# Two grouped-query attention blocks on one core: six K and three V buffers, a wq load moved behind x, 105 remainder tiles transposed by DMA

## The chip, the cores and the metric

The kernel runs on one core of a Trainium2 chip. The metric is the device time of one execution in microseconds (us), as the median of several runs; lower is better.

## The reference

Two independent problems, A and B, have the same shapes: x is (16, 80, 576), wq (576, 4096), wo (4096, 576), and the K and V caches are (16, 16, 512, 128), all bf16. There are 32 query heads on 16 key and value heads, so two query heads share each K and V.

```python
q = (x @ wq).reshape(B, Sq, Hq, Dh).transpose(0, 2, 1, 3)
k = jnp.repeat(k_cache, 2, axis=1); v = jnp.repeat(v_cache, 2, axis=1)
scores = jnp.einsum("bhqd,bhkd->bhqk", q, k) * (Dh ** -0.5)
p = softmax(scores)
o = jnp.einsum("bhqk,bhkd->bhqd", p, v)
y = o.transpose(0, 2, 1, 3).reshape(B, Sq, Hq * Dh) @ wo
# output: concatenate([y_A, y_B], axis=-1)
```

## The kernel before, in words

**Units.** The attention is cut into 128 units U, 64 for each problem. A unit is one batch element and four key heads, and needs one K load and one V load of 512 KB each. Each key head has 2 x 80 = 160 query rows: 128 of them make a main score tile of 128x512, and the 32 left over of all four heads together make a fifth one, the remainder tile. So a unit has five tiles, k = 0 (remainder) to 4.

**The way of a tile.** On TensorE (PE): scores (L713, or L699 for the remainder, which is made for two units at once: 0, 1, then 2 and 3, 4 and 5, and so on); on DVE the negated row maximum (L722); on ACT the exponential with its row sum (L726); on DVE the reciprocal (L732); on POOL the scaling of the probabilities (L735). Then the tile is transposed, on PE by four 128x128 transposes (L741) with a copy out of PSUM (L748 and L750), or, for the remainder tile of the units in the table RSEL, by one DMA transpose from SBUF to SBUF (L754), with no work on PE or DVE. PV (L788, 16 matmuls a unit) multiplies with V, and ACT copies the result into oT (L804).

**Around it.** The query projection (L589) works in octets of eight units; wq comes in slices of 1024 columns, in two buffers. x of problem A is loaded as it stands (L492, four loads: x00 and x01 for the first half of the batch, x10 and x11 for the second) and transposed on PE (L507); x of problem B comes transposed by DMA (L527). The first two wq slices are loaded in two halves each (w00, w01, w10, w11; each half is a 64 KB and a 512 KB load, L560 and L563). The output projection (L841) gathers over pairs of slices, in acc and then into the output (L853, L869, L875).

**What sets the order.** A planner in the kernel (`_Sched`) runs when the kernel is built. Each operation has a stream, a key that is its due time, a duration and, for loads, a cost; `arrange` walks through planned time and gives each engine a fixed list. The chip then follows these lists, with semaphores for what is needed. For the first loads the planner uses landing times from the table LAND; later it models two queues. An operation with `after` does not start, in the plan, before the PV of a given mark (mark 4U + j is the j-th PV group of unit U) has, plus `lag`.

**Queues.** SP issues all loads of K (L663, DMA transposes), x, wq and wo, the remainder transposes (L754) and the stores (L875). ACT issues the V loads from V 4 on (L667). The order of the first loads on SP is the tuple FIRST, then x10, x11, v2 and v3 in LATER.

**Buffers.** K U sits in buffer U modulo NK, V U in U modulo NV, the transposed probabilities in one of NPT = 3. A load waits until PE has read the buffer's last content.

The lines that matter to the loads:

```python
S.add("sp", ... else 5.0 * gfirst[U] + 0.5 * (U - gfirst[U]) - LA - KK, em_ldk, writes=[R(("kT", ks), U)],
      ... after=4 * U - KPH if U >= KU0 else None, ...)
S.add(VENG if U >= NVS else "sp", ... else 5.0 * U - VK, em_ldv, ...
      lag=VLAG if U >= NVS else 0.0, after=... 4 * U - VPH if U >= VU0 else None, ...)
```

Of the kernel before, what the change touches and what calls it, by code (L numbers as in the profile page):

```python
# [11 lines left out]
GRP = (1, 1, 2)  # L12
GR = 2
LA = 13
NK = 5
NV = 4
NPA = 10
NPR = 5
NPT = 3
# [2 lines left out]
QL1 = 11.0  # L22
KC = 2.1
VK = 8.0
KK = 8.0
DLAT = 0.6
XC = 0.4
QL2 = 10.3
VC = 1.75
# [7 lines left out]
NWARM = 8  # L37
NWARM2 = 2
QP1 = (0.4, 1.1)
FIRST = ("x00", "w00", "x01", "w01", "k0", "w10", "k1", "v0", "k2", "k3", "v1", "w11", "k4")  # L40
LATER = dict(x10=-0.40, x11=-0.39, v2=-0.38, v3=-0.37)
LAND = dict(x00=4.1, w00=6.4, x01=8.0, w01=9.6, k0=11.5, w10=14.6, k1=18.1, v0=19.4, k2=21.8, k3=23.7, v1=26.4, w11=28.1,
            k4=30.3, k5=33.0, x10=35.7, x11=36.9, v2=38.0, v3=39.5, k6=43.2, k7=46.8)
NFK = 5
PTX = (0,)
NPX = 128
QEV = {160: dict(act=0.21, dve=0.24), 320: dict(act=0.32, dve=0.40), 480: dict(act=0.43, dve=0.57)}
NWC = 4
BANKS = dict(S=(0, 1, 2, 6), T=(3, 4), O=(5, 7), M=(7, 5), M0=(7, 5, 6, 3, 4), M1=(7, 6), ML=(7, 5, 6, 0, 1))
# [1 line left out]
VENG = "act"  # L51
VDUR = 0.42
VN = 1
VLAG = 2.0
VPH = 11
VU0 = 14
KPH = 27
KU0 = 10
KLAG = 0.0
XM = dict(wo=6.0, wq=6.0, wqb=6.0, RT=4.0, V=2.0, K=2.0, x=3.0)  # L60
# [2 lines left out]
WENG = "sp"  # L63
WOENG = "sp"
WLAG = 2.0
NVS = 4
QLAT = 1.25
QRING = 1.45
WOC = 1.05
XDMA = True  # L70
RG = (((0, 1, 2, 3, 4),), ((0,), (1, 2, 3, 4)))
RSEL = ((14, 15, (0, 1, 2, 3)), (17, 45, (0, 1, 2, 3)), (47, 48, (0, 1, 2, 3)), (49, 50, (0, 1, 2, 3)), (51, 52, (0, 1, 2, 3)), (53, 54, (0, 1, 2, 3)), (55, 56, (0, 1, 2, 3)), (57, 58, (0, 1, 2, 3)), (59, 76, (0, 1, 2, 3)), (77, 78, (0, 1, 2, 3)), (79, 80, (0, 1, 2, 3)), (83, 84, (0, 1, 2, 3)), (85, 88, (0, 1, 2, 3)), (89, 119, (0, 1, 2, 3)), (120, 121, (0, 1, 2, 3)), (122, 123, (0, 1, 2, 3)), (124, 128, (0, 1, 2, 3)))
RDC = 0.72
RDK = 2.0
RDO = 10.0
# [13 lines left out]
LPC = 29.0  # L89
WOR = (((4.0, 1.5), (12.0, 1.5)), ((7.0, 1.6), (15.6, 1.6)), ((8.0, 1.7), (16.0, 1.7)), ((9.0, 1.7), (16.0, 1.4)))  # L90
WQR = (2.0,3.5,9.5)
WQX = {9: (5.0, 2.0), 13: (4.0, 2.0)}
XR = ((-12.0, 1.9), (-9.5, 1.6))

MM0 = 0.0025
MM1 = 1.0 / 2400.0
# [274 lines left out]
def bass_concat_heads__gqa_block_cached__gqa_block_cached__near_ridge_kernel(  # L371
# [27 lines left out]
    with ExitStack() as es:  # L399
# [6 lines left out]
        kT = sb("kT", [128, NK, 4, 512], BF16)  # L406
# [24 lines left out]
        S = _Sched()  # L431

        def R(res, ver):
            return (res, ver)
# [33 lines left out]
        def em_warmend(e):  # L468
# [5 lines left out]
              stream="warmset")  # L474
# [12 lines left out]
        for half in range(NPP):  # L487
            x_ap = probs[0][0]
            for part, (k0, k1) in enumerate(XP):
                def em_ldx(e, x_ap=x_ap, half=half, k0=k0, k1=k1):  # L490
                    src = x_ap.rearrange("b s d -> (b s) d")[half * NROW + k0 * 128:half * NROW + k1 * 128, :]
                    return e.dma_start(xs[:, half * NRT + k0:half * NRT + k1, 0:D],  # L492
                                       src.rearrange("(k p) d -> p k d", p=128))

                S.add("sp", FIRST.index("x%d%d" % (half, part)) - 100.0 if half == 0 else LATER["x%d%d" % (half, part)], em_ldx,
                      writes=[R(("xs", half * NRT + k_), 0) for k_ in range(k0, k1)], dsem="d_x%d%d" % (half, part), land=LAND["x%d%d" % (half, part)],
                      name="ldx%d.%d" % (half, part), stream="later" if half else "first", dur=0.5, cost=XC * (k1 - k0))
            for blk in range(NRT):
                rb = half * NRT + blk
                vb = S.bank("M0" if half == 0 else "M1")  # L500
                x = (XA + 0.5 * blk if blk < 2 else XA + XB + 0.1 * blk) if half == 0 else XH + 0.8 * blk

                def em_xtr(e, rb=rb, vb=vb):
                    last = None
                    for ck in range(5):
                        c0 = ck * 128 if ck < 4 else D - 128
                        last = e.transpose(psb[:, vb.phys, ck * 128:(ck + 1) * 128], xs[:, rb, c0:c0 + 128], ident[:])  # L507
                    return last

                def em_xev(e, en=None, half=half, blk=blk, vb=vb):  # L510
                    return (e.copy if en == "act" or half == 0 and blk in (1, 3) else e.tensor_copy)(xT[:, half, :, blk * 128:(blk + 1) * 128],  # L511
                                         psb[:, vb.phys, 0:640].rearrange("p (c n) -> p c n", c=5))

                S.add("pe", x, em_xtr, reads=[R(("xs", rb), 0), IDENT], writes=[R(vb, 0)], name="xtr%d" % rb,
                      stream="X", dur=_mm(5, 128), lat=0.2, alloc=[vb])
                S.add(("act", "dve") if half else "act" if blk in (1, 3) else "dve", x + 0.3, em_xev, reads=[R(vb, 0)], writes=[R(("xT", half, blk), 0)],
                      name="xev%d" % rb, stream="xed" if half else "xea" if rb in (1, 3) else "xev",
                      dur=dict(act=0.52, dve=0.40), lat=0.13)

        for half in range(NPP):  # L520
            x_ap = probs[1][0]
            st0 = UPR + 16 * half - lead[NG // 2 + 2 * half]
# [16 lines left out]
        for goct in range(NG):  # L539
            prob, q, half = unit(goct)  # L540
# [4 lines left out]
            pieces = () if half else ((0, 512), (512, 1024)) if goct < 2 else ((0, 1024),)  # L545
            for pi, (c0, c1) in enumerate(pieces):
                st0 = u0 - lead[goct]
                t_ld = 5.0 * st0 - 20.0 if goct > 1 else FIRST.index("w%d%d" % (goct, pi)) - 100.0
                dsem = "d_wq%d" % wsl
                eng = "sp" if goct < 2 else WENG  # L550
                strm = "first" if goct < 2 else "wq"
                sp_ = st0 if goct < 2 else u0 - 16 - lead[goct - 2] + max(QSH, lead[goct - 2] - QS0)
                if goct < 2:
                    parts = ((4, 5, c0, c1), (0, 4, c0, c1))
                else:
                    parts = tuple((0, 4, 256 * j, 256 * j + 256) for j in range(4)) + ((4, 5, 0, 1024),)
                for j, (k0, k1, n0, n1) in enumerate(parts):
                    def em_ldw(e, wq_ap=wq_ap, q=q, wsl=wsl, n0=n0, n1=n1, k0=k0, k1=k1):
                        if k0 == 4:
                            return e.dma_start(wq_sb[64:128, wsl, 4, n0:n1],  # L560
                                               wq_ap[512:576, q * 1024 + n0:q * 1024 + n1])
# [12 lines left out]

# [79 lines left out]
        for U in range(NSU):  # L654
# [10 lines left out]
            def em_ldv(e, vc_ap=vc_ap, b=b, q=q, vs=vs):  # L665
                src = vc_ap[b:b + VN, 4 * q:4 * q + 4, :, :].rearrange("b g (p j) d -> p b g (j d)", j=4)
                return e.dma_start(v_sb[:, vs:vs + VN, :, :], src)  # L667

            S.add("sp", FIRST.index("k%d" % U) - 100.0 if U < NFK else 5.0 * gfirst[U] + 0.5 * (U - gfirst[U]) - LA - KK, em_ldk, writes=[R(("kT", ks), U)],
                  dsem="d_k%d" % ks, name="ldk%d" % U, stream="K" if U >= NFK else "first", dur=1.8, cost=KC, xp=True,  # L670
                  after=4 * U - KPH if U >= KU0 else None, lag=KLAG if U >= KU0 else 0.0, land=LAND.get("k%d" % U, 0.0))
            if U % VN == 0:
                S.add(VENG if U >= NVS else "sp", FIRST.index("v%d" % U) - 100.0 if U < 2 else LATER["v%d" % U] if U < NVS else 5.0 * U - VK, em_ldv, writes=[R(("V", vs + i_), U + i_) for i_ in range(VN)],
                      dsem="d_v%d" % vs, name="ldv%d" % U, stream="V" if U >= NVS else "later" if U > 1 else "first", dur=VDUR, cost=VN * VC,
                      lag=VLAG if U >= NVS else 0.0, after=VAF[U] if U < 4 else 4 * U - VPH if U >= VU0 else None,
                      land=LAND.get("v%d" % U, 0.0))

            vo = None
            rdma = any(a_ <= U < b_ and U % 4 in m_ for a_, b_, m_ in RSEL)
            for k in range(5):  # L680
# [91 lines left out]
                else:  # L772
                    S.add("pe", t0, em_tr, reads=[R(("P", psl), ("n", T)), IDENT], writes=[R(vt, 0)],
                          name="tr%d" % T, stream="T", dur=_mm(4, 128), lat=0.2, alloc=[vt])
                    free_ = k in PTX and U < NPX
                    S.add(("act", "dve") if free_ else "dve", t0 + 0.44, em_ptev, reads=[R(vt, 0)], writes=pt_writes,
                          name="ptev%d" % T, stream="ptex" if free_ else "ptev", dur=dict(act=0.50, dve=0.33), lat=0.13, ahead=PTO)

# [176 lines left out]
```

## Time and profile before

| | |
|---|---|
| runs | 764.65, 765.46 and 767.38 us; median 765.46 us |
| the profiled execution | 765.12 us; its span, first to last instruction, 763.4 us |
| TensorE clock granted | 1.000 |
| moved by DMA | 172.86 MB, mean 226 GB/s |
| K loads (L663) | 128; issue 3.58 us (A) and 3.19 us (B) median, landing 4.3 / 6.9 / 10.6 us |
| V loads (L667) | 128; landing 3.8 / 5.1 / 7.8 us |
| remainder transposes (L754) | 94; issue 1.21 us median, landing 2.4 / 4.9 / 8.4 us |

Landing is the time from the start of the issue to the end of the transfer, as minimum / median / maximum.

How to read it: the page's first part is the busy time of each engine with its share of the span and its count of instructions. A matmul's duration contains the drain of the array, which overlaps with the next one, so the pace is read from start to start in the order of time. A number in square brackets is the idle time of the engine before an instruction, followed by what ended it; where the engine named there had long been done, it was another, often a DMA. PEld is the weight load of TensorE, which overlaps with matmuls. SP's issue instructions are not counted as busy.

### The profile page before, as it was taken

To read this page: it belongs to the slowest core of one execution; us is meant where nothing else is said; L and a number is where in the kernel's file an instruction comes from. 1 tells how busy PE (TensorE), PEld (TensorE's weight loads), DVE (VectorE), ACT (ScalarE), POOL (GpSimd) and SP (SyncE) were. 2 spreads that over 40 slices of the span, in tenths; PEclk is the share of its full clock that TensorE was granted. 3 is DMA by queue.
4 is the path that set the end of the run, shared out by engine and by line. 5 is a ranking of instruction groups with operands and counts; after the bars stand their busy time and mean duration, and the time that the engine had idled before them with its cause. 6 is when DMAs were issued, how large, how long until landed. Compare 5 with 4: busy or idle time off the path is not lost.

```text
span 763.4 us, 21017 instructions
## 1 busy us (share of the span) xinstructions
PE 756.6 (99%) x7876; PEld 572.3 (75%) x7876; DVE 676.7 (89%) x1602; ACT 603.7 (79%) x1691; POOL 432.3 (57%) x647
## 2 busy tenths in 40 slices
PE   8999999999999999999999999999999999999998
PEld 4677777777777777777777777777777777777786
DVE  5999999998888898999989999889889989999982
ACT  3878988888888887787887878887888888877860
POOL 1646755656565565565656555655656565564660
PEclk9999999999999999999999999999999999999999
DMA  9999999999998999999999999999999999999751
GB/s 223 261 244 240 244 248 262 233 222 234 196 240 198 255 258 251 261 218 210 241 228 214 226 248 247 240 251 251 234 219 214 199 227 237 226 264 258 182 121 32
DMA packets 431364, 172.86 MB, mean 226 GB/s; under 512 B 327968, under 2 KB 430880, under 8 KB 431264
## 3 DMA queue, kind: packets, MB, share of 16 engines
q1 hardware_dynamic: 365712, 106.43, 78.4%
q10 hardware_dynamic: 65552, 65.09, 28.4%
q8 instruction: 64, 1.05, 0.6%
q14 instruction: 36, 0.29, 0.1%
HBM read 87.46 MB, written 2.95 MB: 118 GB/s over the span
## 4 chain that ended last, share of the span: by engine, by line
PE 97%; DVE 1%; ACT 1%; issue 0%
PE ps L589 23%; PE ps L841 21%; PE ps L788 18%; PE ps L741 16%; PE ps L713 14%; PE ps L699 5%; DVE negmax L722 1%; PE ps L461 0%; ACT p_sb L726 0%; PE ps L507 0%; DVE qT L601 0%; DVE xT L511 0%; ACT qT L600 0%; ACT xT L511 0%; DVE pT L750 0%
## 5 line engine op out<-in xcount | busy, mean ns | idle before, releaser
L735 POOL TENSOR_SCALAR p_sb<-p_sb,rinv 128x512 bf16<-128x512 bf16 x640 | 429.9, 692 | 308.9 <-DVE rinv L732 308.8
L726 ACT ACTIVATE p_sb<-ps,negmax 128x512 bf16<-128x512 f32 x640 | 440.9, 695 | 90.8 <-DVE negmax L722 81.4
L722 DVE TENSOR_REDUCE negmax<-ps 128x1 f32<-128x512 f32 x640 | 425.1, 680 | 17.0 <-PE ps L713 12.2
L788 PE MATMUL ps<-pT,v_sb 128*128 128x160 bf16 x2048 | 221.9, 233 | 0.0
L750 DVE COPY pT<-ps 128x512 bf16<-128x512 bf16 x512 | 206.1, 414 | 11.9 <-PE ps L741 11.2
L589 PE MATMUL ps<-xT,wq_sb 128*128 128x320 bf16 (+2 forms) x1280 | 213.5, 299 | 1.6 <-ACT xT L511 0.7
L741 PE MATMUL ps<-ident,p_sb 128*128 128x128 bf16 x2184 | 209.8, 219 | 0.0
L788 PEld LDWEIGHTS ps<-pT,v_sb 128*128 128x128 bf16 x2048 | 164.6, 98 | 47.7 <-issue 2.1
L713 PE MATMUL ps<-kT,qT 128*128 128x512 bf16 x512 | 193.4, 379 | 0.0
L741 PEld LDWEIGHTS ps<-ident,p_sb 128*128 128x128 bf16 x2184 | 155.1, 98 | 34.4 <-issue 5.1
L841 PE MATMUL ps<-wo_sb,oT 128*128 128x288 bf16 x1280 | 170.0, 286 | 0.0
L589 PEld LDWEIGHTS ps<-xT,wq_sb 128*128 128x128 bf16 x1280 | 116.0, 98 | 52.7 <-DVE qT L601 2.5
L841 PEld LDWEIGHTS ps<-wo_sb,oT 128*128 128x128 bf16 x1280 | 122.4, 98 | 34.6 <-issue 1.7
L804 ACT CAST oT<-ps 128x320 bf16<-128x320 f32 x256 | 109.0, 426 | 29.5 <-PE ps L788 27.9
L726 ACT ACTIVATION_READ_ACCUMULATOR p_sb<-ps,negmax 128x1 f32 x640 | 132.1, 206 | 0.0
L601 DVE TENSOR_SCALAR qT<-ps 128x320 bf16<-128x320 f32 (+2 forms) x158 | 76.5, 485 | 13.8 <-PE ps L589 11.1
L600 ACT ACTIVATE qT<-ps 128x320 bf16<-128x320 f32 x98 | 43.1, 440 | 15.6 <-PE ps L589 15.4
L713 PEld LDWEIGHTS ps<-kT,qT 128*128 128x128 bf16 x512 | 50.0, 98 | 2.8 <-issue 0.2
L732 DVE RECIPROCAL rinv<-rowsum 128x1 f32<-128x1 f32 (+2 forms) x222 | 36.3, 165 | 8.2 <-ACT p_sb L726 8.2
L869 DVE TENSOR_TENSOR osb<-ps,acc 128x288 bf16<-128x288 f32 x40 | 18.3, 457 | 27.1 <-PE ps L841 27.1
L699 PE MATMUL ps<-kT,qT 128*32 128x512 bf16 x512 | 39.6, 384 | 1.0 <-ACT oT L804 0.6
L853 ACT COPY acc<-ps 128x288 f32<-128x288 f32 x40 | 15.9, 397 | 2.9 <-PE ps L841 2.7
(19 smaller groups left out, 46.3 us busy)
## 6 DMA issues: line engine op xcount, KB each, us to landing
v_sb<-in_B_v_cache_dram ACTq DMA_DIRECT2D x64, 512.0 KB, 5.1
v_sb<-in_A_v_cache_dram ACTq DMA_DIRECT2D x60, 512.0 KB, 5.1
wo_sb<-in_A_wo_dram SPq DMA_DIRECT2D x16, 288.0 KB, 5.3
wo_sb<-in_B_wo_dram SPq DMA_DIRECT2D x16, 288.0 KB, 4.6
wq_sb<-in_B_wq_dram SPq DMA_DIRECT2D x16, 256.0 KB, 5.2
out_dram<-osb SPq DMA_DIRECT2D x40, 72.0 KB, 3.4
wq_sb<-in_A_wq_dram SPq DMA_DIRECT2D x4, 512.0 KB, 5.1
v_sb<-in_A_v_cache_dram SPq DMA_DIRECT2D x4, 512.0 KB, 5.4
```

What stands on the lines that cost most here:

```text
L589: last = e.matmul(ps[:, vb.phys, 0:n1 - n0], lhsT=wq_sb[:, wsl, ck, i * 128:(i + 1) * 128], rhs=xT[:, half, ck, n0:n1], start=(ck == 0), s ...
L601: return e.tensor_scalar(dst, src, SCALE, None, op0=AluOpType.mult)
L699: last = e.matmul(ps[32 * g4:32 * g4 + 32, vb_.phys, :], lhsT=qT[:, qp_, g4 * 160 + 128:g4 * 160 + 160], rhs=kT[:, ks_, :, g4 * 128:(g4 + ...
L713: return e.matmul(ps[:, vb.phys, :], lhsT=qT[:, qp, gl * 160:gl * 160 + 128], rhs=kT[:, ks, :, gl * 128:(gl + 1) * 128], start=True, stop= ...
L722: return e.tensor_reduce(negmax[:, si:si + 1], ps[:, vb.phys, :], axis=AX.X, op=AluOpType.max, negate=True)
L726: return e.activation(p_sb[:, psl, :], ps[:, vb.phys, :], AF.Exp, bias=negmax[:, si:si + 1], scale=1.0, accum_out=rowsum[:, ss, k:k + 1])
L735: return e.tensor_scalar(p_sb[:, psl, :], p_sb[:, psl, :], rinv[:, ss, k:k + 1], 1.0, op0=AluOpType.mult, op1=AluOpType.mult)
L741: last = e.transpose(psb[:, vt.phys, j * 128:(j + 1) * 128], p_sb[:, psl, j * 128:(j + 1) * 128], ident[:])
L750: return cp(pT[:, pts, :, 0:4, gl * 32:gl * 32 + 32], psb[:, vt.phys, 0:512].rearrange("p (j h c) -> p j h c", j=4, h=4))
L788: last = e.matmul(ps[:, vo.phys, off:off + 160], lhsT=v_sb[:, vs, gl, j * 128:(j + 1) * 128], rhs=pT[:, pts, j, :, gl * 32:gl * 32 + 32], ...
L804: return e.copy(dst, src)
L841: last = e.matmul(ps[:, vb.phys, 0:DC], lhsT=oT[:, hi, rb * 128:(rb + 1) * 128], rhs=wo_sb[:, hi, c3 * DC:(c3 + 1) * DC], start=(hi == 0), ...
```

## The change

K gets a sixth buffer and V loses one of four (the two have the same size). K loads may be issued earlier (KPH, KK), V's plan terms follow the smaller number (VPH, VLAG). The first loads get a new order: K 4 and K 5 go ahead, then V 2, x10, x11 and w11; V 3 goes to ACT's queue. RSEL covers eleven more units: 15, 16, 45, 52, 54, 81, 82, 84, 119, 121 and 123. x of problem B is issued a little sooner (XR), and one wq slice loses its delay (WQX). The line numbers grow by two from L492 on.

```diff
-NK = 5
-NV = 4
+NK = 6
+NV = 3
...
-KK = 8.0
+KK = 13.0
...
-FIRST = ("x00", "w00", "x01", "w01", "k0", "w10", "k1", "v0", "k2", "k3", "v1", "w11", "k4")
-LATER = dict(x10=-0.40, x11=-0.39, v2=-0.38, v3=-0.37)
-LAND = dict(x00=4.1, w00=6.4, x01=8.0, w01=9.6, k0=11.5, w10=14.6, k1=18.1, v0=19.4, k2=21.8, k3=23.7, v1=26.4, w11=28.1,
-            k4=30.3, k5=33.0, x10=35.7, x11=36.9, v2=38.0, v3=39.5, k6=43.2, k7=46.8)
-NFK = 5
+FIRST = ("x00", "w00", "x01", "w01", "k0", "w10", "k1", "v0", "k2", "k3", "v1", "k4", "k5")
+LATER = ("v2", "x10", "x11", "w11")
+FKEY = dict([(n_, i_ - 100.0) for i_, n_ in enumerate(FIRST)] + [(n_, 0.05 * i_ - 0.49) for i_, n_ in enumerate(LATER)])
+LAND = dict(x00=4.1, w00=6.4, x01=8.0, w01=9.6, k0=11.5, w10=14.5, k1=18.0, v0=19.3, k2=21.8, k3=23.7, v1=26.4, k4=28.7,
+            k5=31.4, v2=33.2, x10=34.4, x11=36.0, w11=37.7, v3=39.4, k6=43.2, k7=46.5)
+NFK = 6
 PTX = (0,)
-NPX = 128
+PTY = (1,)
+NPY = 0
...
-VLAG = 2.0
-VPH = 11
+VLAG = 0.5
+VPH = 9
...
-KPH = 27
+KPH = 31
...
-NVS = 4
+NVS = 3
...
-RSEL = ((14, 15, ...), (17, 45, ...), (47, 48, ...), ... (124, 128, ...))
+RSEL = ((14, 46, ...), (47, 48, ...), (49, 50, ...), (51, 56, ...), (57, 58, ...), (59, 76, ...), (77, 78, ...), (79, 80, ...), (81, 88, ...), (89, 128, ...))
...
-WQX = {9: (5.0, 2.0), 13: (4.0, 2.0)}
-XR = ((-12.0, 1.9), (-9.5, 1.6))
+WQX = {13: (4.0, 2.0)}
+XR = ((-12.0, 1.7), (-12.0, 1.6))
...
-                    free_ = k in PTX and U < NPX
+                    free_ = k in PTX or k in PTY and U < NPY
```

The other changed lines only look the keys up in FKEY.

More of the change, by code (lines that the diff above doesn't have):

```diff
@@ L71 @@
 RG = (((0, 1, 2, 3, 4),), ((0,), (1, 2, 3, 4)))
-RSEL = ((14, 15, (0, 1, 2, 3)), (17, 45, (0, 1, 2, 3)), (47, 48, (0, 1, 2, 3)), (49, 50, (0, 1, 2, 3)), (51, 52, (0, 1, 2, 3)), (53, 54, (0, 1, 2, 3)), (55, 56, (0, 1, 2, 3)), (57, 58, (0, 1, 2, 3)), (59, 76, (0, 1, 2, 3)), (77, 78, (0, 1, 2, 3)), (79, 80, (0, 1, 2, 3)), (83, 84, (0, 1, 2, 3)), (85, 88, (0, 1, 2, 3)), (89, 119, (0, 1, 2, 3)), (120, 121, (0, 1, 2, 3)), (122, 123, (0, 1, 2, 3)), (124, 128, (0, 1, 2, 3)))
+RSEL = ((14, 46, (0, 1, 2, 3)), (47, 48, (0, 1, 2, 3)), (49, 50, (0, 1, 2, 3)), (51, 56, (0, 1, 2, 3)), (57, 58, (0, 1, 2, 3)), (59, 76, (0, 1, 2, 3)), (77, 78, (0, 1, 2, 3)), (79, 80, (0, 1, 2, 3)), (81, 88, (0, 1, 2, 3)), (89, 128, (0, 1, 2, 3)))
 RDC = 0.72
@@ L493, in em_ldx @@
                                        src.rearrange("(k p) d -> p k d", p=128))
-                S.add("sp", FIRST.index("x%d%d" % (half, part)) - 100.0 if half == 0 else LATER["x%d%d" % (half, part)], em_ldx,
+                S.add("sp", FKEY["x%d%d" % (half, part)], em_ldx,
                       writes=[R(("xs", half * NRT + k_), 0) for k_ in range(k0, k1)], dsem="d_x%d%d" % (half, part), land=LAND["x%d%d" % (half, part)],
-                      name="ldx%d.%d" % (half, part), stream="later" if half else "first", dur=0.5, cost=XC * (k1 - k0))
+                      name="ldx%d.%d" % (half, part), stream="first", dur=0.5, cost=XC * (k1 - k0))
             for blk in range(NRT):
@@ L547, in bass_concat_heads__gqa_block_cached__gqa_block_cached__near_ridge_kernel @@
                 st0 = u0 - lead[goct]
-                t_ld = 5.0 * st0 - 20.0 if goct > 1 else FIRST.index("w%d%d" % (goct, pi)) - 100.0
+                t_ld = 5.0 * st0 - 20.0 if goct > 1 else FKEY["w%d%d" % (goct, pi)]
                 dsem = "d_wq%d" % wsl
@@ L667, in em_ldv @@
                 return e.dma_start(v_sb[:, vs:vs + VN, :, :], src)
-            S.add("sp", FIRST.index("k%d" % U) - 100.0 if U < NFK else 5.0 * gfirst[U] + 0.5 * (U - gfirst[U]) - LA - KK, em_ldk, writes=[R(("kT", ks), U)],
+            S.add("sp", FKEY["k%d" % U] if U < NFK else 5.0 * gfirst[U] + 0.5 * (U - gfirst[U]) - LA - KK, em_ldk, writes=[R(("kT", ks), U)],
                   dsem="d_k%d" % ks, name="ldk%d" % U, stream="K" if U >= NFK else "first", dur=1.8, cost=KC, xp=True,
@@ L672, in bass_concat_heads__gqa_block_cached__gqa_block_cached__near_ridge_kernel @@
             if U % VN == 0:
-                S.add(VENG if U >= NVS else "sp", FIRST.index("v%d" % U) - 100.0 if U < 2 else LATER["v%d" % U] if U < NVS else 5.0 * U - VK, em_ldv, writes=[R(("V", vs + i_), U + i_) for i_ in range(VN)],
-                      dsem="d_v%d" % vs, name="ldv%d" % U, stream="V" if U >= NVS else "later" if U > 1 else "first", dur=VDUR, cost=VN * VC,
+                S.add(VENG if U >= NVS else "sp", FKEY["v%d" % U] if U < NVS else 5.0 * U - VK, em_ldv, writes=[R(("V", vs + i_), U + i_) for i_ in range(VN)],
+                      dsem="d_v%d" % vs, name="ldv%d" % U, stream="V" if U >= NVS else "first", dur=VDUR, cost=VN * VC,
                       lag=VLAG if U >= NVS else 0.0, after=VAF[U] if U < 4 else 4 * U - VPH if U >= VU0 else None,
```

## The prediction

> **What bounds the kernel now.** I read the busy table first, then the chain that ended last, then the table by stretches, and only then the order of time on TensorE (PE).
>
> ```profile
> PE 756.6 (99%) x7876; PEld 572.3 (75%) x7876; DVE 676.7 (89%) x1602; ACT 603.7 (79%) x1691; POOL 432.3 (57%) x647
> ...
> DMA  9999999999998999999999999999999999999751
> ...
> PE 97%; DVE 1%; ACT 1%; issue 0%
> ```
>
> PE is busy in 756.6 of 763.4 us and makes 97% of the chain, so the time is PE's list of matmuls plus its few waits. The DMA engines are full too, until the last slices: there is no room for careless transfers. Stretches (columns: us, then busy us and count of PE, PEld, DVE, ACT, POOL, the clock, DMA share, GB/s):
>
> ```profile
> 0.00:20.00 20.00, 17.31 (x125) 9.56 (x126) 11.36 (x25) 6.88 (x14) 2.44 (x7) 1.00 0.94 226
> 20.00:40.00 20.00, 18.88 (x197) 13.03 (x194) 19.76 (x45) 17.79 (x50) 13.43 (x20) 1.00 1.11 243
> 40.00:60.00 20.00, 19.98 (x201) 14.36 (x198) 19.22 (x46) 14.95 (x43) 10.08 (x15) 1.00 1.18 245
> ...
> 400.00:420.00 20.00, 19.62 (x201) 15.02 (x200) 17.50 (x42) 14.90 (x43) 12.82 (x20) 1.00 1.22 220
> ```
>
> PE loses time only before 40 us (2.69 + 1.12 us) and once at 400 to 420 (0.38 us). All other stretches up to 760 read 20.00. Two of these waits concern the change (start, length, engine, line, shape):
>
> ```profile
> 27.28 0.39 PE L741 MATMUL ps<-ident,p_sb 128*128 128x128 bf16 x4
> 27.50 0.38 PE L713 MATMUL ps<-kT,qT 128*128 128x512 bf16 x1
> ...
> 32.58 0.44 PE L788 MATMUL ps<-pT,v_sb 128*128 128x160 bf16 x4
> 33.60 0.61 PE L699 MATMUL ps<-kT,qT 128*32 128x512 bf16 x8 [0.59 <-ACT oT L804]
> ```
>
> The first pair is the price of one transposed tile: the next instruction starts 27.50 - 27.28 = 0.22 us after four transposes began (0.39 contains the drain, which overlaps). The second pair is a wait: four PV matmuls take 0.275 us start to start elsewhere (27.94 to 28.22), so PE was ready at 32.86 and began at 33.60, 0.74 us late. The view names ACT, but this instruction is the remainder scores of units 4 and 5, and K 5's load, issued at 27.9, took 5.6 us to land: 33.5. It is K 5 that PE waited for. The other one, in the middle:
>
> ```profile
> 406.90 0.84 PE L589 MATMUL ps<-xT,wq_sb 128*128 128x320 bf16 x5
> 408.12 0.61 PE L699 MATMUL ps<-kT,qT 128*32 128x512 bf16 x8 [0.38 <-issue]
> ```
>
> Five 320-column matmuls take 0.68 us (28.22 to 28.89 elsewhere), so PE was ready at 407.58 and lost 0.54 us. These are units 70 and 71, and K 71's load lands at 399.3 + 8.8 = 408.1, just then (the view of that one load; its columns: issue time of SP in ns, first and last start, then the landing):
>
> ```profile
> L663 SPq DMA_TRANSPOSE kT<-in_B_k_cache_dram x1: 2537/2537/2537, 399.3 to 399.3; - x1
> ...
> DMA to landing us min/median/max: 8.8/8.8/8.8
> ```
>
> Again it is K that is late.
>
> **The change part by part**, against the profiled execution (765.12 us, of it the span 763.4; the other 1.7 us stay).
>
> *105 remainder tiles by DMA instead of 94.* Units 15, 16, 45, 52, 54, 81, 82, 84, 119, 121 and 123 are added. Built, the program has 7832 matmuls instead of 7876: 44 fewer, 11 tiles of four. On PE that is 11 x 0.22 = **-2.42 us**, all on the path, since PE reads 20.00 of 20 where these units stand (the first of the 94 transposes, unit 14's, is issued at 95.5 us; unit 15 follows). The copies they spare (L748, 0.41 to 0.59 us each on DVE or ACT) are off the path and worth nothing. Rule against row: the Trainium skill's "TensorE: Matmul & The Clock Gate", Back-to-back issue gap, gives about 81 ns per matmul at 128 columns in a real stream of weight loads and matmuls; by it the term would be 44 x 0.081 = 3.56 us (an estimate from that page). The trace's 55 ns speaks against it.
>
> What the eleven add: each is one more DMA transpose on SP's queue (1.21 us of issue, median of the 94) and 128 KB on the DMA engines. Waiting behind it are K loads, wq, wo and the stores. Can they bear it? In 530 to 665 us every unit but one (units 89 to 118) already has such a transpose, PE reads 135.00 of 135, and the K loads land in 8.8 us at most. So where the queues are as there, one more costs 0, hidden beside PE. The risk is in units 81 to 84: SP is in DMA instructions for 97% of 410 to 530 us. If the cover is gone, the cost there is three times 1.21 us of SP, at most 3.6 us if no K load had any lead; K 81 landed 2.4 us before use, so up to 1.2 us would be left. I take 0, because of the next part.
>
> *Six K buffers, and K issued earlier.* Line 671 lets K U start at mark 4U-31 instead of 4U-27, which is one unit (about 5.6 us: 763 us less head and tail over 128) earlier, and that is what the sixth buffer allows. The late K loads of 71 and 81 (leads 0 and 2.4 us) get up to that much more. K 71's wait goes: **-0.54 us**. Ends: 0 if the queue is full there anyway, 0.54 if not. What is late next is a remainder transpose: unit 68's landed 1.8 us before its PV. I take 0.54, as a lead of one unit is ten times the wait.
>
> *Three V buffers.* In the order of ACT, V U stands at the same place as before: after about 5U+4 exps. In the trace V was issued a median 5.3 us after its buffer came free, about one unit: the fourth buffer was hardly used. From the last PV of unit U-3 to the first of U lie 10.4 us at least (median 13.6), and a V load lands in 3.8 to 7.8 us. So 10.4 - 7.8 = 2.6 us are left in the worst pair: cost 0. V's issue sits in ACT's queue behind the copy that follows that same PV, so no wait is added. If ACT slipped by over 2.6 us, PV would wait; the largest ACT instruction is 0.7 us. V 3 moves from SP to ACT, whose next user comes at about 45 us: 0.
>
> *The head.* w11 (64 + 512 KB) held SP from 22.18 to 23.37 ahead of K 4, and landed 1.7 us after V 1. Behind x, it lets K 4 and K 5 start 1.2 us sooner and land 1.2 to 1.7 us sooner: K 5 at 31.8 to 32.3, before PE's 32.86. Gone are 0.74 us. What is late next: V 2 now goes ahead of x, about 2.0 us of transfer (37.4 against 35.4 in the trace), then x10 (0.8) and x11 (1.1): x10 lands at 34.6 to 35.1, x11 at 35.7 to 36.2, w11 at 37.4 to 37.9. In the new order PE reaches the x transposes one tile earlier, at 35.38 - 0.74 = 34.64: a wait of 0 to 0.5 us. The projections on w11 come 2.6 + 0.7 us later, at 37.9: 0. K 7, with a lead of 1.0 us, gets about 0.5 us more PE work before its first use and asks for nothing. Ends: -0.24 (x late) and -0.74 - 0.78 (the three smaller waits at 37.1, 38.5 and 41.0, 0.31 + 0.28 + 0.19, vanish too, as x is no longer between scores). DVE, at 19.76 of 20 us there, speaks against the latter. I take **-0.5**.
>
> *The rest.* The flag on the remainder's copies leaves them free to go to ACT or DVE, as before (NPY is 0 and adds none). x of problem B is issued up to 2.5 units sooner and wq of one octet without its delay: transfers moved, none added, cost 0, and up to +0.5 us if they collide with the K loads at 400 us.
>
> Sum: -2.42 - 0.54 - 0.5 = -3.46; 765.12 - 3.46 = 761.66. The median of the runs shown is 0.34 above the profiled execution, so **762.0 us**.
>
> **Rivals.**
> - *Only the transposes count*: x takes K 5's place in the head, K 71 stays late. For: both are DMA landings on full engines. Against: w11's 1.2 us are plainly out of K's way. 765.46 - 2.42 = 763.0.
> - *The gain comes back as DMA waits*: a dozen landings with 0.2 us each missing, as ready tiles on PE run out. For: DVE at 98% in 60 to 100 us. Against: PE reads 20.00 there, and the removed copies unload DVE. About 765.
> - *Slower: SP's queue between 350 and 530 us runs dry of time.* Leads of K fall there from 16.5 us (unit 64) to 0.3 (unit 71): 16.2 over 7 units, 2.3 us a unit, while x, wq, wo and stores of both problems share the queue. If the three transposes of units 81 to 84 and the earlier x turn that stretch into a lasting deficit, each further K is 2.3 us late once the lead is used up; the sixth buffer gives 5.6 us, and it decides from the third unit. Three late units cost 6.9 us: 763.0 + 6.9 = 769.9. Against: the lead was back at 10 us by unit 76. Named beside it: the Trainium skill's "DMA: Bandwidth & Descriptors", Specifications, puts line rate at transfers of 512 B or more; here 327968 of 431364 packets are smaller, and the rule speaks against adding more of them; no trace here shows the cost of a packet by its size.
> - *A transpose is paced by its weight load*: that row (L741 on PEld) has 98 ns, so a tile would cost 0.39 us, the term be -4.31, and the time 760.1. The 0.22 us per four speak against it. The Trainium skill's page on TensorE, cited above, lies between the two.
> - *It doesn't do what it says*: the built order shows 44 matmuls fewer and K 5's load without a wait, so only a landing can spoil it.
>
> **How the numbers follow.** Forecast 0.56 (760.7 to 762.9), only the transposes 0.20 (762.7 to 763.6), given back 0.12, slower 0.09, weight loads 0.03. A run can be told from no change beyond 0.3%, that is 2.3 us: faster is below 763.2. Faster: 0.56 + 0.03 + half of 0.20 = 0.69; slower 0.09; the same 0.22. The range goes from all head waits gone (761.66 - 1.0 = 760.6, a little less for spread) to the start of the case where the gain comes back: 760.3 to 764.7.
>
> **What would show it.** Right: PE has 7832 matmuls and about 2.4 us less work; no wait ahead of L701 at 32 to 34 us; 400 to 420 us reads 20.00; leads of K in units 64 to 81 grow by several us; no V load lands later than 1 us before its PV. Wrong: a wait before the x transposes (L509) of over 0.5 us, a stretch between 300 and 530 us with PE under 19.5, or remainder transposes (L756) landing after PE is ready.

## The result and the profile after

The changed kernel takes 776.93 us (median of four runs, 774.21 to 784.45) where the kernel before takes 765.16 in the same comparison: a ratio of 1.0143, 95% interval 1.0102 to 1.0183. It is slower by 11.8 us, and the forecast was 762.0. The profiled execution took 776.47 us, with a span of 774.7 (before: 765.12 and 763.4).

The page of the kernel after: busy times, the DMA row of the 40 slices, and the chain that ended last.

```profile
PE 759.3 (98%) x7832; PEld 572.5 (74%) x7832; DVE 674.9 (87%) x1605; ACT 604.6 (78%) x1688; POOL 434.3 (56%) x647
...
DMA  8999999999999999999999999999999999999951
...
PE 84%; DMA 7%; DVE 4%; SPq 4%; ACT 1%; issue 0%; POOL 0%
```

The 44 matmuls are gone, yet PE is busy 2.7 us longer, and DMA and SP's queue now stand in the chain, where before PE had 97% of it. The stretches of the kernel after (us, then busy us and count of PE, PEld, DVE, ACT, POOL, clock, DMA share, GB/s):

```profile
20.00:40.00 20.00, 19.18 (x192) 12.94 (x191) 19.05 (x43) 18.25 (x51) 13.49 (x20) 1.00 1.07 226
40.00:60.00 20.00, 17.45 (x164) 12.71 (x163) 15.57 (x35) 13.20 (x39) 7.30 (x11) 0.91 1.17 228
...
340.00:360.00 20.00, 17.32 (x170) 12.90 (x167) 14.36 (x34) 12.34 (x34) 9.33 (x14) 0.91 1.10 210
...
400.00:420.00 20.00, 20.00 (x208) 14.96 (x206) 17.68 (x43) 16.16 (x47) 10.12 (x16) 1.00 1.10 223
```

Before 40 us PE loses 0.8 us less than before, and 400 to 420 is full, as forecast. But 40 to 60 and 340 to 360 lose 2.6 and 2.7 us of PE each, and in both the granted clock is 0.91: after the wait TensorE ran at half its clock for 3.41 us (from 50.12 and from 347.08), which costs another 1.7 us each. What PE waited for (the list of waits of the kernel after; total us, times, longest):

```profile
PE ps L790 <- DMA pT<-p_sb: 5.6, 5, 2.7
PE ps L701 <- DMA kT<-in_A_k_cache_dram: 2.5, 1, 2.5
...
PE ps L790 <- ACT p_sb L728: 0.9, 1, 0.9
```

One K load, and five remainder transposes. The 0.9 us put down to ACT are a sixth one: PV of unit 18 starts at 134.36, and its transpose lands at 134.27. With a wait of 0.2 us for unit 84's it is 6.7 us in seven waits.

**The K load.** PE in order of time in the kernel after, first where K 5 made it wait before, then where it waits now:

```profile
32.71 0.44 PE L790 MATMUL ps<-pT,v_sb 128*128 128x160 bf16 x4
33.08 0.61 PE L701 MATMUL ps<-kT,qT 128*32 128x512 bf16 x8
...
46.70 0.44 PE L790 MATMUL ps<-pT,v_sb 128*128 128x160 bf16 x4
49.68 0.66 PE L701 MATMUL ps<-kT,qT 128*32 128x512 bf16 x8 [2.55 <-DMA kT<-in_A_k_cache_dram]
50.27 1.51 PE L591 MATMUL ps<-xT,wq_sb 128*128 128x320 bf16 x5
```

and the scores of the second place in the kernel before, where nothing makes them wait:

```profile
47.08 0.61 PE L699 MATMUL ps<-kT,qT 128*32 128x512 bf16 x8
```

K 5's wait is gone. The remainder scores of units 6 and 7 wait instead, and the five matmuls behind them take 1.51 us where 0.84 is usual: the half clock. K 7 was issued at 37.89 and landed at 49.64, after 11.8 us; before, it was issued at 39.59 and landed after 6.7. K 6 (12.1 us; before 10.5) and V 3 (10.6 us on ACT's queue) are slow with it. The loads of V 3 and K 7 in the kernel after:

```profile
L669 ACTq DMA_DIRECT2D v_sb<-in_A_v_cache_dram x1: 394/394/394, 33.1 to 33.1; - x1
...
DMA to landing us min/median/max: 10.6/10.6/10.6
```

```profile
L665 SPq DMA_TRANSPOSE kT<-in_A_k_cache_dram x1: 5467/5467/5467, 37.9 to 37.9; - x1
...
DMA to landing us min/median/max: 11.8/11.8/11.8
```

**The transposes.** The longest of these waits, on PE in the kernel after:

```profile
344.03 0.40 PE L743 MATMUL ps<-ident,p_sb 128*128 128x128 bf16 x4
347.11 0.69 PE L790 MATMUL ps<-pT,v_sb 128*128 128x160 bf16 x4 [2.68 <-DMA pT<-p_sb]
```

and SP's queue ahead of it (start, length of the issue, instruction):

```profile
328.70 5.74 SPq L665 DMA_TRANSPOSE kT<-in_A_k_cache_dram  x1
334.55 1.23 SPq L756 DMA_TRANSPOSE pT<-p_sb  x1
335.82 2.81 SPq L665 DMA_TRANSPOSE kT<-in_A_k_cache_dram  x1
338.67 0.58 SPq L877 DMA_DIRECT2D out_dram<-osb  x1
339.30 0.43 SPq L630 DMA_DIRECT2D wo_sb<-in_A_wo_dram  x1
339.83 1.81 SPq L756 DMA_TRANSPOSE pT<-p_sb  x1
```

The last line is unit 55's transpose. In the kernel before it is this one:

```profile
328.14 1.19 SPq L754 DMA_TRANSPOSE pT<-p_sb  x1
```

In the kernel after it starts the moment SP has issued a K load, unit 54's transpose (one of the eleven), a second K load, a store and a wo load. It lands 7.1 us later, at 346.97, and PV starts at 347.11. SP issues in order, so a transpose that could start stands behind whatever is ahead of it. How long can be read: it could start when POOL has scaled its tile and the PV of three units earlier has left its buffer (three buffers for the transposed probabilities). For unit 55 that is 331.50, 8.3 us before its issue, and SP is issuing in 8.0 of them; in the kernel before it is 0.9 us (327.20 to 328.14). Over all transposes this time in the queue has a median of 0.4 us before (mean 1.3) and 5.0 after (mean 4.6). In both kernels SP spends about 95% of these delays issuing, mostly K loads, so it was busy and not waiting for a buffer. PV comes about 13.1 us after that point in both kernels (median). The six waits over 0.3 us had 4.8 to 8.5 us in the queue and then landings of 5.6 to 8.9 us, so most of the delay is the queue's and a smaller part the landing's.

Two simpler readings agree. In the trace before, 55 of 94 start within 0.15 us of the end of another instruction on SP, so the queue and not their data held them; after, 91 of 105. From issue to first use lie 12.2 us before (median; least 6.7) and 8.3 after (least 4.6). The landing itself is the same: 4.9 and 5.0 us median.

### The profile page after: what moved, and what is told of

It reads as the page before. It is cut to its first block, busy times and chain, and to the rows that moved or that the text cites. A ratio compares the mean times of both kernels' runs of the same rounds, so it can differ in the third digit from the quotient of the medians.

```text
span 774.7 us, 20933 instructions
## 1 busy us (share of the span) xinstructions
PE 759.3 (98%) x7832; PEld 572.5 (74%) x7832; DVE 674.9 (87%) x1605; ACT 604.6 (78%) x1688; POOL 434.3 (56%) x647
## 4 chain that ended last, share of the span: by engine, by line
PE 84%; DMA 7%; DVE 4%; SPq 4%; ACT 1%; issue 0%; POOL 0%
PE ps L843 20%; PE ps L591 18%; PE ps L790 17%; PE ps L743 14%; PE ps L715 12%; DMA pT<-p_sb 5%; PE ps L701 4%; SPq L665 3%; DVE negmax L724 2%; DMA kT<-in_A_k_cache_dram 2%; DVE pT L752 1%; DMA acc<-in_A_x_dram 1%; DVE qT L603 1%; ACT p_sb L728 0%; POOL p_sb L737 0%
## 5 line engine op out<-in xcount | busy, mean ns | idle before, releaser
L743 PE MATMUL ps<-ident,p_sb 128*128 128x128 bf16 x2140 | 205.8, 220 | 0.0
L743 PEld LDWEIGHTS ps<-ident,p_sb 128*128 128x128 bf16 x2140 | 152.9, 98 | 33.4 <-issue 6.8
L734 DVE RECIPROCAL rinv<-rowsum 128x4 f32<-128x4 f32 (+2 forms) x233 | 37.7, 163 | 8.0 <-ACT p_sb L728 8.0
```

The costliest lines, as they stand in the source:

```text
L743: last = e.transpose(psb[:, vt.phys, j * 128:(j + 1) * 128], p_sb[:, psl, j * 128:(j + 1) * 128], ident[:])
```

## The experiments

Three theories for the loss. **1**: K loads, issued one unit earlier, stand ahead of the transposes in SP's queue. In the built order 90 of the 94 transposes before stood behind the K of four units later, and 100 of the 105 after stand behind that of five units later. **2**: the eleven more transposes are what SP's queue cannot bear, wherever K stands. **3**: three V buffers, which make V loads collide with K.

The first four, on one chip (before: 765.59 us): each part undone or done alone.

*K issued as late as before (six buffers kept).*

```diff
-KK = 13.0
+KK = 8.0
-KPH = 31
+KPH = 27
```

> The kernel after with the plan terms of K as before (KPH 27, KK 8); six K and three V buffers, the new head and the 105 tiles stay. Theory 1 (earlier K loads fill SP's queue, and remainder transposes that are ready stand behind them, 91 of 105 issued at once behind another SP instruction, against 55 of 94 before): the share falls to about 60%, the waits of PE on pT between 100 and 600 us go (some 7 us of lost PE time), and what is left is the head's wait for K 7 with its cold clock: 766 to 769 us. Theory 2 (the eleven more tiles are too much for SP and the DMA engines): 774 to 777, as after. Theory 3 (three V buffers make V loads start just as the buffer comes free and collide with the transposes): 774 to 777.

Measured: 769.67 us, ratio 1.0048 [1.0009, 1.0087], span 766.6. The share held up by the queue falls from 0.87 to 0.70. K 7 still costs 1.7 us, and PV waits twice in the middle, until 132.19 and 145.03 us, for 1.4 and 1.6. The view names other engines there, but transposes land at 132.10 and 144.94: it is they. With a third of 0.3 their cost goes from 6.7 to 3.4 us. Early K is a part, not all.

*The 94 tiles of before in the kernel after.*

```diff
-RSEL = ((14, 46, ...), (47, 48, ...), ... (89, 128, ...))
+RSEL = ((14, 15, ...), (17, 45, ...), ... (124, 128, ...))
```

> The kernel after with the 94 tiles of before. Theory 1 (K loads ahead of ready transposes): the waits stay and PE has 2.4 us more work, 775 to 779 us; 85% or more of the 94 transposes still issued at once behind another SP instruction. Theory 2 (too many tiles): most waits go, 765 to 769. Theory 3 (V): 775 to 779.

Measured: 771.5 us, ratio 1.0035 [0.9992, 1.0077], span 772.1. Two lines of this kernel, one of PE in order of time and one of the stretches:

```profile
53.79 1.04 PE L701 MATMUL ps<-kT,qT 128*32 128x512 bf16 x8 [6.91 <-DMA kT<-in_A_k_cache_dram]
```

```profile
340.00:360.00 20.00, 20.00 (x211) 15.10 (x209) 18.14 (x44) 16.34 (x46) 11.13 (x18) 1.00 1.21 246
```

The middle is full: early K with 94 tiles makes no transpose late. Theory 1 by itself falls. The head is worse still: K 7 lands 16.1 us after its issue, PE waits 6.91 us, and the clock is halved for 6.83 us, from 1.9 us before the wait ends. No edit of this kernel touches the head, so that loss belongs to what it shares with the kernel after, and its size varies.

*The 105 tiles in the kernel before* (RSEL the other way).

> The kernel before with the 105 tiles alone. Theory 1 (K loads ahead): SP keeps its slack, 44 matmuls fewer show as 2.4 us: 762.5 to 764 us, PE 20.00 of 20 in nearly all stretches. Theory 2 (too many tiles): 768 to 775, waits on pT. Theory 3 (V): 762.5 to 764.

Measured: 768.21 us, ratio 1.0002 [0.9956, 1.0047], span 765.3. PV waits until 303.74, 336.20 and 343.17 us, for 0.7, 0.8 and 1.85; transposes land at 303.65, 336.07 and 343.08. So theory 2 holds in kind: the eleven tiles make transposes late with K at its old place too. In size it gives no loss: 3.6 us of waits (a fourth is 0.25) against 2.42 saved, and no measurable change.

*Three V buffers in the kernel before, V 3 on ACT.*

```diff
-NV = 4
+NV = 3
-LATER = dict(x10=-0.40, x11=-0.39, v2=-0.38, v3=-0.37)
+LATER = dict(x10=-0.40, x11=-0.39, v2=-0.38)
-VLAG = 2.0
-VPH = 11
-NVS = 4
+VLAG = 0.5
+VPH = 9
+NVS = 3
```

> The kernel before with three V buffers (V 3 issued by ACT, V's plan terms as after), five K buffers and 94 tiles. Theory 1 (K loads ahead) and theory 2 (tiles): 765 to 767 after the head; if V 3 on ACT's queue is what slowed the loads of K 6 and K 7 in the head, a wait of 1 to 3 us appears at 47 to 50 us, 767 to 769. Theory 3 (V): waits on pT or V through the whole run, 770 to 776.

Measured: 769.17 us, ratio 1.0059 [1.0026, 1.0091], span 774.0. PE in order of time, the remainder scores of units 6 and 7:

```profile
50.89 1.04 PE L699 MATMUL ps<-kT,qT 128*32 128x512 bf16 x8 [3.28 <-issue]
```

The same wait as after, in the kernel before, from the V part alone: K 6, V 3 and K 7 land after 12.9, 11.5 and 12.7 us. Behind 60 us only one wait for a transpose (2.43 us) remains. So theory 3 holds for the head, and hardly elsewhere. In time the V part alone is 4.5 us (0.0059 of 765.59).

What moved in the head is V 3: from SP, in line with K 6 and K 7, to ACT, beside them. The next four kernels (one chip, before: 767.47 us) put it back on SP.

*V 3 on SP's queue ahead of K 6.*

```diff
+FKEY["v3"] = 7.0
-NVS = 3
+NVS = 4
...
-after=4 * U - KPH if U >= KU0 else None, lag=KLAG if U >= KU0 else 0.0
+after=4 * U - KPH if U >= KU0 else 3 if U == 6 else None, lag=KLAG if U >= KU0 else 0.6
...
-cost=VN * VC,
+cost=VN * VC, ahead=10.0 if U == 3 else 0.0,
```

> The kernel after with V 3 back on SP's queue, between w11 and K 6 (K 6 starts, in the plan, behind unit 0's last PV). Theory H (the head's wait for K 7 comes from V 3 on ACT's queue, whose packets mix with those of K 6: K 6 and V 3 took 12 and 11 us to land, and K 7 12): K 6 and K 7 land in under 11 and 8 us, the wait of 1.7 to 6.9 us at 47 to 54 us and its cold clock are gone, 3 to 8 us less than after; the waits on pT from 100 to 600 us stay: 769 to 773 us. Rival (the head's wait comes from the new order of K 4, K 5, V 2, x and w11 alone): the wait stays, 774 to 780.

Measured: 770.06 us, ratio 1.0025 [0.9985, 1.0064], span 772.8. A stretch of this kernel, then its list of waits:

```profile
40.00:60.00 20.00, 20.00 (x207) 14.60 (x205) 18.65 (x43) 16.01 (x47) 10.08 (x15) 1.00 1.20 236
```

```profile
PE ps L791 <- DMA pT<-p_sb: 10.0, 8, 2.6
```

The head's wait is gone: K 6 and K 7 land after 10.5 and 6.8 us. Over all profiles of this study, the five with V 3 on ACT have K 7 landing after 11.8 to 16.1 us and PE waiting 1.7 to 6.9 us for it; the eleven with V 3 on SP have 6.7 to 8.2 us and no wait over 0.3 there. So V 3's move is the cause, as the edits in both directions show. It changes two things at once, the queue of V 3 and its place (issued behind K 6 instead of ahead of it); which of them does it was not run apart. What is left is the transposes, in this execution 10.6 us in ten waits, eight of them in the list; 92 of 105 were held up by the queue.

*The same with 94 tiles.*

> The kernel after with V 3 on SP and the 94 tiles of before. If the head (V 3) and the eleven tiles are all that makes after slower: no wait of PE after 45 us, K 71 without its wait, 762.5 to 765 us. If earlier K loads alone put transposes too far back in SP's queue: waits on pT remain, 767 to 771.

Measured: 765.32 us, ratio 0.9978 [0.9948, 1.0008], span 763.2; one wait of 0.4 us for a transpose, 65 of 94 held up. Both causes are out, and the kernel is where before is.

*V 3 on SP, 105 tiles, K as late as before.*

> The kernel after with V 3 on SP and K's plan terms as before (KPH 27, KK 8), 105 tiles. Tiles as the cause: some waits on pT and K remain, as in the kernel before with 105 tiles (5 transposes and 5 K loads with a lead under 0.6 us there): 764 to 768. Earlier K as the cause: none remain, 761 to 763.

Measured: 770.11 us, ratio 1.0037 [0.9995, 1.0079], span 767.2. 81 of 105 held up. This is above what either theory gave. The transposes cost 1.9 us, but 4.4 us go to remainder scores, which start at 339.43 and 355.21 us; K loads land at 339.34 and 355.12. With 105 tiles SP is late either way; the order only chooses between K and the transposes, and in time the two orders are the same (1.0037 and 1.0025).

*V 3 on SP, 105 tiles, early K; the 40 stores and the 32 wo loads issued by ACT.*

```diff
-STENG = "sp"
+STENG = "act"
-WOENG = "sp"
+WOENG = "act"
```

> The kernel after with V 3 on SP, and the 40 stores and 32 wo loads issued by ACT instead of SP (72 instructions of 0.6 us, 43 us of SP's time; the DMA engines move the same bytes). If SP's queue in order is what makes transposes late: the share issued at once behind another SP instruction falls from 0.87 to under 0.75, waits on pT mostly go, 762 to 766 us unless ACT, 78% busy, becomes late itself. If it is the DMA engines' rate: the waits stay, 769 to 773.

Measured: 768.32 us, ratio 0.9997 [0.9952, 1.0042], profiled span 762.3. The whole list of waits of PE over 0.3 us:

```profile
PE ps L464 <- DVE wo_sb L454: 1.2, 1, 1.2
PE ps L592 <- DVE xT L514: 0.6, 1, 0.6
PE ps L716 <- ACT p_sb L729: 0.4, 1, 0.4
```

No wait for a transpose. 67 of 105 are held up, from issue to use lie 12.1 us again, and the time that a transpose stands in the queue falls from 4.7 to 0.7 us (median), with the same bytes on the DMA engines. So in this execution 72 issues of about half a microsecond, moved off SP, do it. It is one of the three fastest of ten, though: the ten spread from 762.4 to 773.5, six of them had a stretch at half clock, as many as with the issues on SP, and the ratios 0.9997 and 1.0025 are not told apart. That this edit ends the waits in most executions is not shown.

Four more (before: 765.50 us) ask how much of this is SP alone.

*The kernel after once more.*

> The kernel after once more, for its spread beside the variants on one chip. Both causes (V 3 on ACT in the head; transposes late in SP's queue) are in it: median 772 to 778 us, runs from 766 to 785.

Measured: 774.69 us, ratio 1.0097 [1.0063, 1.0130], span 772.7. The head's wait is 2.2 us, others of 1.6 and 2.1 us come later; 79 of 105 held up. The pattern repeats, its places in the middle only in part: units 63, 90 and 91 wait in both profiles.

*The kernel before with 105 tiles, stores and wo on ACT.*

> The kernel before with the 105 tiles, and the stores and wo loads issued by ACT (43 us of issue off SP). If late transposes come from SP's queue: the 105 tiles then give their 2.4 us, 761.5 to 764 us, no wait on pT. If from the DMA engines: as with the 105 tiles alone, median 2 to 3 us above before.

Measured: 769.31 us, ratio 1.0045 [1.0013, 1.0077], span 765.3. A miss: PE waits 1.0 and 0.8 us for transposes that land at 264.92 and 272.55, and 1.65 us for a K load that lands at 284.54; 70 of 105 are held up. The time in the queue does fall against the 105 tiles alone, from 4.1 to 1.9 us (median), the kernel's time does not. Relieving SP was not enough here, with K late.

*Early K, V 3 on SP, 94 tiles, stores and wo on ACT.*

> The kernel after with V 3 on SP, the 94 tiles, stores and wo loads on ACT: what is left of the change is the sixth K buffer and the head. If SP's queue was the only trouble: 763 to 765 us with a smaller spread than before. If ACT's queue now delays V or the exponentials: 766 and over, waits of PE on V or S banks.

Measured: 766.53 us, ratio 1.0018 [0.9983, 1.0053], span 763.6, 49 of 94 held up. That is above the 763 to 765 expected with SP as the only trouble, yet no wait on V or on a transpose is in its profile; the interval includes 1, so nothing is gained or lost.

*The kernel before, stores and wo on ACT (the control).*

> The kernel before with only the stores and wo loads moved to ACT, as a control: PE's work is the same, K 71 may lose its wait of 0.54 us: 764 to 765.5 us, as before. Over 767 would mean that ACT's queue has a cost of its own.

Measured: 766.78 us, ratio 1.0008 [0.9983, 1.0034], span 765.4. K 71 keeps its wait, 1.1 us in this profile. Moving the 72 issues is worth nothing where the transposes are not late.

The last two (before: 765.27 us) split the eleven tiles by where they stand, both with V 3 on SP and early K.

*Five tiles: units 15, 16, 119, 121, 123.*

```diff
-RSEL = ((14, 46, ...), ... (51, 56, ...), ... (81, 88, ...), ...)
+RSEL = ((14, 45, ...), ... (51, 52, ...), (53, 54, ...), (55, 56, ...), ... (83, 84, ...), (85, 88, ...), ...)
```

> The kernel after with V 3 on SP and 99 tiles by DMA: the 94 of before and units 15, 16, 119, 121 and 123. If the place decides: no new waits, 5 x 0.22 = 1.1 us less than with 94, 763 to 765 us and faster than before. If the sum decides: about half of the loss of the 105, 766 to 768.

Measured: 763.79 us, ratio 0.9985 [0.9964, 1.0005], span 761.8. The list of waits and the stretch that was worst:

```profile
PE ps L464 <- DVE wo_sb L454: 1.2, 1, 1.2
PE ps L592 <- DVE xT L514: 0.6, 1, 0.6
PE ps L592 <- DVE qT L604: 0.3, 1, 0.3
```

```profile
340.00:360.00 20.00, 19.95 (x209) 15.21 (x207) 18.84 (x48) 16.05 (x45) 10.94 (x17) 1.00 1.02 230
```

56 of 99 held up, no transpose under 9.1 us from issue to use. The best version of the study, 1.5 us under before, though the interval reaches 1.

*Six tiles: units 45, 52, 54, 81, 82, 84.*

```diff
-RSEL = ((14, 46, ...), ... (89, 128, ...))
+RSEL = ((14, 15, ...), (17, 46, ...), ... (89, 119, ...), (120, 121, ...), (122, 123, ...), (124, 128, ...))
```

> The kernel after with V 3 on SP and 100 tiles by DMA: the 94 of before and units 45, 52, 54, 81, 82 and 84. If the place decides: waits on pT between 290 and 400 us and at 500 to 580 us as with the 105, 768 to 772 us. If the sum decides: about half of them, 766 to 768.

Measured: 765.57 us, ratio 1.0008 [0.9988, 1.0028], span 765.2. The line of its transposes in the list of waits:

```profile
PE ps L791 <- DMA pT<-p_sb: 3.1, 4, 1.8
```

76 of 100 are held up. Below both expectations: the place matters in the profiles, in time the two versions are hardly told apart (their intervals overlap).

Side by side (held up: share of the transposes that SP's queue held; queue: median time in us from when a transpose could start to its issue; waits: idle time of PE, in us, that ends with the landing of the transpose it needs, each over 0.15; clock: executions with a granted clock of 1.00, of all). Everything but the ratio and the clock is from one profiled execution each:

| kernel | V 3 | K | tiles | 72 issues | held up | queue | waits | ratio | clock |
|---|---|---|---|---|---|---|---|---|---|
| before | SP | late | 94 | SP | 0.59 | 0.4 | 0 | 1 | 98 of 113 |
| after, first set | ACT | early | 105 | SP | 0.87 | 5.0 | 6.7 | 1.0143 | 0 of 4 |
| after, second set | ACT | early | 105 | SP | 0.75 | 2.4 | 6.8 | 1.0097 | 1 of 10 |
| 94 tiles | ACT | early | 94 | SP | 0.63 | 0.7 | 0 | 1.0035 | 2 of 10 |
| K late | ACT | late | 105 | SP | 0.70 | 1.3 | 3.4 | 1.0048 | 4 of 10 |
| before, 105 tiles | SP | late | 105 | SP | 0.78 | 4.1 | 3.6 | 1.0002 | 6 of 10 |
| before, three V buffers | ACT | late | 94 | SP | 0.69 | 0.9 | 2.4 | 1.0059 | 7 of 10 |
| V 3 on SP | SP | early | 105 | SP | 0.88 | 4.7 | 10.6 | 1.0025 | 4 of 10 |
| V 3 on SP, 94 tiles | SP | early | 94 | SP | 0.69 | 0.6 | 0.4 | 0.9978 | 7 of 10 |
| V 3 on SP, K late | SP | late | 105 | SP | 0.77 | 2.3 | 1.9 | 1.0037 | 3 of 7 |
| V 3 on SP, issues on ACT | SP | early | 105 | ACT | 0.64 | 0.7 | 0 | 0.9997 | 4 of 10 |
| V 3 on SP, issues on ACT, 94 tiles | SP | early | 94 | ACT | 0.52 | 0.1 | 0 | 1.0018 | 7 of 10 |
| before, 105 tiles, issues on ACT | SP | late | 105 | ACT | 0.67 | 1.9 | 1.8 | 1.0045 | 3 of 10 |
| before, issues on ACT | SP | late | 94 | ACT | 0.47 | 0.0 | 0 | 1.0008 | 9 of 10 |
| V 3 on SP, 99 tiles | SP | early | 99 | SP | 0.57 | 0.2 | 0 | 0.9985 | 11 of 12 |
| V 3 on SP, 100 tiles | SP | early | 100 | SP | 0.76 | 2.1 | 3.1 | 1.0008 | 10 of 12 |

## Why the prediction was wrong, step by step

**44 fewer matmuls, -2.42 us: right as a term.** The count is 7832, and with V 3 on SP the kernel with five of the eleven tiles has a span of 761.8 against 763.2 with none of them, of which 0.4 are a wait: 1.0 is left where five tiles were to give 1.1. The term lacked its price on SP.

**"Where the queues are as there, one more costs 0", and "I take 0, because of the next part": this step failed.** It put the eleven issues on SP at nothing. It was argued from units 89 to 118, where every unit but one has such a transpose and nothing waits. But there a transpose that could start was issued after 0.03 us (median), so the row shows a queue with time to spare, and the eleven stand elsewhere. After the change the queue is late before that stretch begins, and units 90 and 91, inside it, wait themselves (554.38 and 560.24 us). Those who pay are not the added tiles: of 39 such waits in the profiles with 100 or 105 tiles, two are for added ones. And the step took the cover for the eleven from "the next part", the sixth K buffer. The two parts do not cover each other, they use the same queue. With 94 tiles, early K costs 0.4 us of waits (V 3 on SP, ratio 0.9978); with 105 tiles and late K they are 3.6 us (before, 1.0002); both together give 6.7 (after) and 10.6 (V 3 on SP). K's lead did grow (unit 71 from 0.3 to 9.3 us, unit 81 from 2.4 to 9.0): SP's time was taken from the transposes and given to K. The prediction had named them, "What is late next is a remainder transpose: unit 68's landed 1.8 us before its PV", and then gave them no price. Two of its signs of being wrong came: a stretch between 300 and 530 us with PE under 19.5 (17.32), and remainder transposes that land after PE is ready. Its slower rival had SP's queue and a stretch near the right one, but with K as what comes late.

**"V 3 moves from SP to ACT, whose next user comes at about 45 us: 0" and "K 7 ... asks for nothing": these failed as well.** ACT had the time; the two transfers did not. V 3 on ACT was issued at 33.06, 1.3 us after K 6, and ran beside it, where before SP issued it 0.6 us ahead of K 6. From 37 to 50 us, the stretch of the kernel before and that of the kernel after:

```profile
37.00:50.00 13.00, 12.75 (x132) 9.31 (x133) 12.58 (x31) 9.80 (x28) 8.56 (x13) 1.00 1.18 256
```

```profile
37.00:50.00 13.00, 10.38 (x111) 7.65 (x108) 9.96 (x23) 9.32 (x26) 8.49 (x14) 1.00 1.24 180
```

The DMA engines are as busy as before and move 180 instead of 256 GB/s. With V 3 on SP it is 242; with 94 tiles and V 3 on ACT, 146. The rate alone does not tell the two apart, though: with V 3 on SP and the 72 issues on ACT it was 189, and K 7 landed after 7.9 us. When K 7 and V 4 are issued at 38 us, K 6 and V 3 are still in transfer (until 43.9 and 43.6): four loads of 512 KB at once, where before there were three, K 6, V 4 and K 7. The step took K 7's landing of 6.7 us from the trace; the nearest row for a load that starts behind others still in transfer was K 6's, 10.5 us, and with it K 7 would have been expected at 48.4, behind PE at 47.1.

**K 5, K 71 and the rest of the head: right, the size in part by luck.** K 5's wait of 0.74 us is gone, the x transposes wait 0.36 us, inside 0 to 0.5, and K 71's wait is gone. Before 40 us PE lost 3.05 us instead of 3.81, so -0.76 where -0.5 was taken; but 0.46 of it fell before 20 us, where the change moves no load, and 20 to 40 us gave 0.30, near the weak end of 0.24. **Three V buffers in the steady state, cost 0: right**; the least V lead of the profile after is 2.3 us (1.1 in its second set).

**The sum.** Against the span of before, 11.3 us are to be placed. PE's idle time after 40 us adds 9.7, the two stretches at half clock 3.4; the 44 matmuls give back 2.4, the head 0.8, and the small waits of before 0.4. That is 9.5. Some 1.8 us are left. By estimate more than 1 us of it belongs to the waits themselves: one is about 0.15 us longer from start to start than its idle time (0.74 and 0.59 us for K 5 in the prediction), and the kernel after has nine of over 0.1 us behind 40 us. The rest is not placed. By the ratios the V part alone costs 4.5 us in the kernel before, and the eleven tiles 3.6 with V 3 on SP (1.0025 less 0.9978); their sum of 8.1 stands against 9.2 and 11.8 us in the two sets of the kernel after. Each of these is uncertain by some 3 us.

**What stays open.** Why K 6 and K 7 land so late with V 3 on ACT, and why the DMA rate falls, is seen, not explained. The 128 K issues, the largest user of SP's time, take 446 to 491 us in the sixteen profiles, so an issue gets longer in some of them; whether what is in transfer makes it so, and SP's time thus hangs on the DMA engines in part, was not tried. Nor do the runs say which transposes come late in a given execution: the two profiles of the kernel after share only some places. The ratios of the single steps overlap in part; that the waits end where their cause is removed rests on the profiles, one for each kernel.

## What to carry to other kernels

Price an added DMA by the time of the queue that issues it, together with everything else that the same change moves ahead in that queue: a longer lead for one user of an in-order queue is a shorter one for the next. Measure the leads of all its users, not only that of the one that is late today, and the time between when each could start and when it is issued. A stretch where the queue has time to spare does not price an addition elsewhere. And a load moved to an idle engine's queue is not free: look for what is in transfer at that moment.

## What the runs showed of the hardware

**A wait of 2.1 us can bring the half clock.** In the kernel after, 3.41 us at a granted clock of 0.5 follow waits of 2.55 and 2.68 us, in its second set one of 2.06. Others of 2.26 and 2.98 us, in two kernels with V 3 on SP, had none. The traces show what decides: the starts of the half-clock stretches of a trace lie whole steps of 3.413 us apart (50.12 and 347.08 are 87 steps), so they lie on a fixed grid. At full clock a stretch follows where PE was idle for 2.05 us or more within one step (2.05, 2.19, 2.40, 2.55, 2.66 and 3.41 us, in the middle of four runs), and none follows up to 2.00. The wait of 2.98 was split by the grid into 1.41 and 1.56, that of 2.26 into 0.26 and 2.00. These idle times rest on matmul ends that the profile models. The Trainium skill's "TensorE: Matmul & The Clock Gate", Part 1, has the array cold after at least one idle window of about 3.4 us, in a window that runs freely. The length of 3.41 us and the fixed grid agree; here a step that was idle for 2.05 us of it sufficed.

**The mean clock of an execution tells what it lost.** Of 113 executions of the kernel before, 98 have a clock of 1.00 and a median of 765.41 us; seven have 0.998, which is one such stretch (1 - 0.5 x 3.41 / 763), and a median of 769.8. One stretch thus goes with 4.4 us: 1.7 at half clock, and the rest is about the wait that it takes to bring it. All but one of the 14 executions of the kernel after have at least one.

**SP's issue time was scarce.** SP spends 659 of 763 us issuing before and 705 of 775 after; 128 K issues take 454 us of SP before and 489 after, and a remainder transpose takes 1.21 us to issue and 4.9 to land (medians). The Trainium skill's "DMA: Bandwidth & Descriptors", Issuing engines are not separate DMA queues, says that issuing from several engines only saves the sequencer's time, which it calls usually small. It was not small here: in the profiles, 72 issues moved to ACT took the time in the queue from 4.7 to 0.7 us and the waits for transposes from 10.6 us to none, though the ten runs show no clear gain in time. That section also has DMAs from all engines run on the same 16 DMA engines and interleave; the landing of 11.8 us for K 7, beside V 3 and V 4 from ACT, agrees.
